# Layer two of a two-layer mixture of experts: four weight gathers issued one at a time, a later gate product, and a last strip in three slices

## The chip, the cores and the metric

One core of one Trainium2 chip runs the whole program. The metric is device time in microseconds of one execution. A core has a tensor engine (TensorE, PE in the profile), a vector engine (VectorE, DVE), a scalar engine (ScalarE, ACT), GpSimd (POOL) and a queue engine (SyncE, SP); each runs its own instructions in order, and they wait for one another by semaphores. Transfers run on the core's 16 DMA engines. In this kernel SP issues the plain and transposing transfers and POOL the indirect ones (gathers and scatters).

## The reference, cut to what matters

```python
def reference(**kwargs):
    attn_out = _attn_ref(**attn_kwargs)            # (4, 8, 576, 64), local and strided masks
    x = attn_out.transpose(0, 2, 1, 3).reshape(2304, 512)
    x = _moe_ref(x=x, **moe_kwargs)                # layer one: every token through all 8 experts
    return _moe2_ref(x=x, **moe2_kwargs)           # layer two: every token through one expert

def _moe2_ref(x, w_gate, w1, w2):                  # N = 2304, D = 512, E = 8, F = 1024
    cap = N // E                                   # 288 tokens for each expert
    logits = x @ w_gate
    order = np.argsort(-logits.flatten())
    for idx in order:                              # greedy: best free (token, expert) pair first
        tok, e = idx // E, idx % E
        if assigned[tok] >= 0 or counts[e] >= cap:
            continue
        assigned[tok] = e
        counts[e] += 1
    for e in range(E):
        h = np.maximum(x[assigned == e] @ w1[e], 0.0)
        out[assigned == e] = h @ w2[e]
    return out
```

The greedy assignment is done in rounds. A round (`route`) finds which expert fills up next, by a search over the sorted keys, and closes it. So the order of the experts is known only while the kernel runs, and each expert's weights and rows are fetched by indirect transfers whose index a round has computed.

## The kernel before, in words

Products in both layers work on pairs of two-byte values: a number is split into a high and a low part, and a product is three matmuls (high with high, low with high, high with low).

**Layer one, and the gate product.** Most of the time goes to layer one's experts. `Sides` runs side work between PE's matmuls by planned time: a generator yields (DVE time, ACT time, planned wait), and is taken up again when the planned clock has passed the wait. One of these generators is `late_tiles`, which begins with `late_w`: it multiplies the last expert's second weight with layer two's gate weight, in 8 pieces, adds the two parts (line 1265), takes the largest magnitude of each partition (line 1267) and passes it to `power_max`, whose matmul (line 1040) spreads it over the partitions. The result scales the product, and the last expert of layer one uses it. PE's order is fixed by hand there, so that matmul stands at the place where the generator's wait of 2.5 put it.

**Layer two.** `ffn` runs eight expert phases of 288 rows, in the order in which the rounds deliver the experts. A phase has two parts:
- eight strips `f` of the first product: 12 matmuls of 288 columns (line 1719), then a Relu on ScalarE out of PSUM (line 1724), a copy on ScalarE that makes the high part (line 1725), and a subtraction on VectorE that makes the low part (line 1726);
- four output strips `d` of the second product: 24 matmuls of 288 columns (line 1752) and a copy out of PSUM on ScalarE (line 1760).

In strips 1 to 3 of a phase, `ffn_y` finishes the phase before: for each of three blocks of 96 rows four transposes on PE (line 1692), a scaling copy on ScalarE (line 1694) and a scatter to the output issued by POOL (line 1695). The last phase's three blocks follow behind its last strip.

**Weights and rows of the next expert.** There are three sets of weight buffers, `w3`; phase `ph` uses set `ph % 3` and fetches for phase `ph + 1`. `load_w2` (line 1605) issues four indirect gathers, one for each weight part: high and low of w1, high and low of w2, each 128 rows of 4096 two-byte values. It is called once in a phase, after the first strip at which the next expert's index `wis[ph + 1]` is there (at the latest in strip 5). The rows come by `ffn_g` (three gathers of 96 rows, `g`), called at output strip 1, and go through transposing transfers on SP into `xg` (line 1635), which the next phase's first matmul reads. For phases 6 and 7 PE transposes them instead (line 1639, `ptg`).

**Order of the work.** PE's order in layer two is written out by hand: the program's own order, with the routing's matmuls (`pcnt`, `pany`, `pgg`, `pidx`) put between the strips' matmuls by fixed waits. The other engines' orders are chosen when the program is built, from the dependencies and modelled times. POOL's gathers of weights depend on the index and on nothing of the phase in which they are called. The matmuls' banks in PSUM (`mm`) come from four buffers, the transposes' from two.

Of the kernel before, what the change touches and what calls it, by code (L numbers as in the profile page):

```python
# [13 lines left out]
AF = mybir.ActivationFunctionType  # L14
# [4 lines left out]
N, DM, E, F = 2304, 512, 8, 1024  # L19
CAP = N // E  # L20
WIN = 32
DC = DM // 128
FC = F // 128
# [52 lines left out]
LATE_AT = 8  # L76
DIRECT = 14, 15
TURNED = range(1, 6)


class Arena:
# [14 lines left out]
    def part(self, shape, dt):  # L96
        n = math.prod(shape[1:]) * mybir.dt.size(dt)
        n = (n + 31) // 32 * 32
        r = next(x for x in self.room if x[1] + n <= x[0].shape[1] * 2)
        o, r[1] = r[1] // 2, r[1] + n  # L100
        v = r[0][:shape[0], o:o + n // 2]
        v = (v if dt == F16 else v.bitcast(dt))[:, 0:math.prod(shape[1:])]
        names = "abcd"[:len(shape) - 1]
        return v if len(shape) == 2 else v.rearrange(f"p ({' '.join(names)}) -> p {' '.join(names)}",
                                                     **dict(zip(names[1:], shape[2:])))
# [132 lines left out]
class Kernel:  # L238
# [21 lines left out]
    def bank(self, name, tag="bank"):  # L260
        tag = tag if tag in self.banks else "l1"
        return self.psum.tile([128, 512], F32, name=name, tag=tag, bufs=self.banks[tag])
# [985 lines left out]
    def late_w(self):  # L1248

        nc = self.nc  # L1250
        while ("moe", E - 1, 1) not in self.sides.done:
            yield 0, 0, 0.5
        self.lwp = self.m2.tile([128, FC, 2 * E], F32, name="lwp")
        for c in range(FC):
            t = self.m2.tile([128, 2 * DC, 128], F16, name="turned")
            for k in range(2):
                nc.sync.dma_start(out=t[:, k * DC:k * DC + DC], in_=self.w7d[k][:, c * DM:c * DM + DM], transpose=True)
            yield 0, 0, 8.0
            ps = self.bank("pl", "l1")
            self.gate_dot(ps, (t, t[:, DC:]))  # L1260
            yield 0, 0, 1.0
            nc.scalar.activation(self.lwp[:, c], ps[:, 0:2 * E], AF.Copy)
            yield 0, 0.3, 0
        v = self.lwp[:, :, 0:E]
        nc.vector.tensor_tensor(v, v, self.lwp[:, :, E:], op=OP.add)
        mx = self.sm.tile([128, 1], F32, name="gmx")
        nc.vector.tensor_reduce(mx, v, axis=AX.XY, op=OP.max, apply_absolute_value=True)
        yield 0.5, 0, 2.5
        yield from self.power_max(mx)
        s, self.lwi = self.pow2_scale(self.m2, 8.0, self.top, "lscale")  # L1270
        self.lw = self.m2.tile([128, FC, 2 * E], F16, name="lw")
        self.w_split(v, s[:, 0:1], self.lw[:, :, 0:E], self.lw[:, :, E:])
        yield 1.0, 0, 0
# [328 lines left out]
                t = next(routes, None)  # L1602
                self.wait = 1e9 if t is None else self.wait + t

    def load_w2(self, ph):
        for k in range(4):
            self.nc.gpsimd.indirect_dma_start(out=self.w3[ph % 3][k].rearrange("p a b -> p (a b)"), out_offset=None,
                                              in_=self.wd[k],
                                              in_offset=bass.IndirectOffsetOnAxis(ap=self.wis[ph][:, :1], axis=0))

    def ffn_g(self, ph):

        nc = self.nc
        idx = self.places[ph][0]
        gs = []
        for s in range(3):
            if ph:
                g = self.fp.tile([96, XR], F16, name=f"g{s}")
            else:
                g = self.r0.tile([96, XR], F16, name=f"g{s}", bufs=1)  # L1620
            nc.gpsimd.indirect_dma_start(out=g, out_offset=None, in_=self.xd,
                                         in_offset=bass.IndirectOffsetOnAxis(ap=idx[:, s:s + 1], axis=0))
            gs.append(g)
        self.gs[ph] = gs

    def ffn_x(self, ph, s):
# [6 lines left out]
        xg, osc = self.fx[ph]  # L1633
        if ph in TURNED:
            nc.sync.dma_start(out=xg[:, :, s * M:s * M + M], in_=gs[s][:, 0:2 * DM], transpose=True)
# [66 lines left out]
    def ffn(self, routes):  # L1702

        nc, fp = self.nc, self.fp
        bank = lambda: self.bank("mm", "l1")[:, :CAP]
        for ph in range(E):
            w = self.w3[ph % 3]
            if ph + 1 < E:
                loaded = False
            xg = self.fx[ph][0]  # L1710
            hh = fp.tile([128, FC, CAP], F16, name="h2h")
            hl = fp.tile([128, FC, CAP], F16, name="h2l")
            for f in range(FC):
                ps = bank()
                fs = slice(f * 128, f * 128 + 128)
                k = 0
                for d in range(DC):
                    for l, r in ((w[0], d), (w[0], DC + d), (w[1], d)):
                        nc.tensor.matmul(ps, l[:, d, fs], xg[:, r], start=k == 0, stop=k == 3 * DC - 1)  # L1719
                        k += 1  # L1720
                    if d == 1:
                        yield
                r = fp.tile([128, CAP], F32, name="h2", bufs=5)
                nc.scalar.activation(r, ps, AF.Relu)
                nc.scalar.activation(hh[:, f], r, AF.Copy)
                nc.vector.tensor_tensor(hl[:, f], r, hh[:, f], op=OP.subtract)
                yield
                if ph and 0 < f < 4:
                    self.ffn_y(ph - 1, f - 1)
                if ph + 1 < E and not loaded:  # L1730
                    if f == 5:
                        self.until_has(self.wis, ph + 1, routes)
                    if len(self.wis) > ph + 1:
                        self.load_w2(ph + 1)
                        loaded = True
            yt = self.fy[ph] = fp.tile([128, DC, CAP], F32, name="yt")
            for d in range(DC):
                if ph + 1 < E and d == 1:
                    self.until_has(self.places, ph + 1, routes)
                    if ph + 1 not in self.gs:  # L1740
                        self.ffn_g(ph + 1)
                    if ph + 1 in TURNED:
                        for n in range(3):
                            self.ffn_x(ph + 1, n)
                if ph + 1 < E and ph + 1 not in TURNED and d == 3:
                    self.ffn_x(ph + 1, 1)
                ps = bank()
                dsl = slice(d * 128, d * 128 + 128)
                k = 0
                for f in range(FC):  # L1750
                    for l, r in ((w[2], hh), (w[3], hh), (w[2], hl)):
                        nc.tensor.matmul(ps, l[:, f, dsl], r[:, f], start=k == 0, stop=k == 3 * FC - 1)  # L1752
                        k += 1
                    if f % 2 and f < FC - 1:
                        if ph + 1 < E and ph + 1 not in TURNED and (d, f) in ((2, 5), (3, 3)):
                            self.ffn_x(ph + 1, 2 * d - 4)
                        if ph + 1 == len(self.places) < min(len(self.wis), E):
                            self.spare()
                        yield
                nc.scalar.activation(yt[:, d], ps, AF.Copy)  # L1760
                yield
        for s in range(3):
            self.ffn_y(E - 1, s)

    def layers(self):
        tc, nc = self.tc, self.nc
# [236 lines left out]
```

## Time and profile before

| | |
|---|---|
| time, median of 3 runs | 1873.65 us (1871.69 to 1874.94) |
| the profiled execution | 1867.06 us |
| its span in the trace | 1864.9 us |
| TensorE busy | 1783.4 us, 96% of the span |
| VectorE, ScalarE, GpSimd busy | 60%, 49%, 30% |
| mean rate of the DMA queues | 127 GB/s |
| bytes of POOL's indirect transfers (queue 0) | 43.01 MB |

The span runs from the first to the last instruction in the trace; the device time holds the start and the end around it, 2.2 us here. Shares of busy time are means over the whole span. Layer two's expert phases lie between about 1594 and 1852 us.

### The profile page before, as it was taken

What the parts mean: (1) busy time and instruction counts of PE and PEld (TensorE: products, weight loads), DVE (VectorE), ACT (ScalarE), POOL (GpSimd) and SP (SyncE); (2) the same over time, 40 slices, a digit from 0 to 9 for tenths busy, and PEclk for the clock granted to TensorE, in tenths of its full rate; (3) what the DMA queues carried; (4) which work ended last, traced back from release to release, by engine and by line L of the source; (5) the groups of instructions that cost most, each with busy time, mean ns of one, the idle gap of its engine ahead of it and who ended that gap; (6) DMA issues with size and microseconds to landing.
All of it is one profiled execution on the core that took longest, in us unless ns stands there. A gap on an engine that the chain in (4) does not pass through costs nothing.

```text
span 1864.9 us, 32915 instructions
## 1 busy us (share of the span) xinstructions
PE 1783.4 (96%) x12741; PEld 1081.7 (58%) x12741; DVE 1125.2 (60%) x2706; ACT 907.3 (49%) x2145; POOL 550.2 (30%) x557
## 2 busy tenths in 40 slices
PE   6899999999999999999999999999999999888897
PEld 4666765555455555555554555555556764676776
DVE  6744458866766475566536664666545668766630
ACT  5655533563575456456724744376735531232243
POOL 2121202240442134232402331233356513232231
PEclk8899999999999999999999999999999999999999
DMA  8121012232474046406742542466531113465460
GB/s 265 40 70 41 26 46 80 95 125 109 160 238 155 34 158 226 136 35 204 225 125 88 185 132 99 151 205 201 161 113 35 35 46 130 136 200 169 147 232 26
DMA packets 116561, 237.16 MB, mean 127 GB/s; under 512 B 48620, under 2 KB 53300, under 8 KB 108180
## 3 DMA queue, kind: packets, MB, share of 16 engines
q1 hardware_dynamic: 108724, 192.05, 32.1%
q0 software_dynamic: 7680, 43.01, 6.4%
q8 instruction: 100, 1.64, 0.4%
q14 instruction: 57, 0.47, 0.1%
HBM read 160.75 MB, written 64.50 MB: 121 GB/s over the span
## 4 chain that ended last, share of the span: by engine, by line
PE 60%; issue 15%; DVE 12%; ACT 5%; DMA 4%; POOL 2%; another core or an unknown queue 1%; SPq 0%; POOLq 0%; ACTq 0%; DVEq 0%
PE l L1103 22%; PE l L1159 16%; PE l L679 7%; PE mm L1719 3%; PE l L661 3%; PE mm L1752 3%; DVE w1s L547 2%; POOL raw L1012 1%; ACT sm L417 1%; DVE wmx L1059 1%; DMA raw<-in_moe_w_dram 1%; PE po L458 1%; PE pcnt L1384 1%; PE ps L392 1%; DMA ws0h<-m2h 1%
## 5 line engine op out<-in xcount | busy, mean ns | idle before, releaser
L1103 PEld LDWEIGHTS <-w1s 128*128 128x128 f16 x3864 | 370.2, 98 | 210.9 <-issue 4.2
L1103 PE MATMUL l<-sx,w1s 128*128 128x384 f16 (+2 forms) x2208 | 337.3, 312 | 1.3 <-ACT vV L1118 1.1
L1159 PE MATMUL l<-w2h,hl 128*128 128x512 f16 x864 | 327.4, 379 | 0.0
L1159 PE MATMUL l<-w2l,hh 128*128 128x512 f16 x864 | 327.4, 379 | 0.0
L1159 PE MATMUL l<-w2h,hh 128*128 128x512 f16 x864 | 327.4, 379 | 0.0
L551 POOL TENSOR_TENSOR m2l<-raw,m2h 128x512 f16<-128x512 f32 x176 | 206.3, 1173 | 398.6 <-ACT raw L550 348.5
L1159 PEld LDWEIGHTS <-hh 128*128 128x128 f16 x1728 | 167.7, 98 | 197.4
L1103 PE MATMUL l<-xh,w1s 128*128 128x384 f16 (+2 forms) x1104 | 258.7, 312 | 3.5 <-DVE hl L951 2.0
L711 DVE SCALAR_TENSOR_TENSOR acc<-l,pe,acc 128x512 f32<-128x512 f32 x126 | 94.1, 748 | 180.1 <-PE l L1159 154.1
L1012 POOL TENSOR_TENSOR raw<-raw 128x256 f32<-128x256 f32 x112 | 100.0, 896 | 323.1 <-DVE w1s L547 243.6
L1059 DVE TENSOR_REDUCE wmx<-raw 128x1 f32<-128x512 f32 x240 | 152.0, 677 | 45.4 <-DMA raw<-in_moe_w_dram 44.9
L1103 PE MATMUL l<-xl,w1s 128*128 128x384 f16 (+2 forms) x552 | 171.3, 312 | 0.0
L549 ACT ACTIVATE m2h<-raw,wscale 128x512 f16<-128x512 f32 x176 | 125.3, 712 | 91.1 <-DVE wscale L287 36.6
L1159 PEld LDWEIGHTS <-hl 128*128 128x128 f16 x864 | 84.5, 98 | 102.0
L1118 ACT ACTIVATE vV<-l 128x384 f32<-128x384 f32 x144 | 68.4, 488 | 132.3 <-PE l L1103 131.5
L550 ACT ACTIVATE raw<-raw,wscale 128x512 f32<-128x512 f32 x176 | 127.0, 722 | 5.7
L679 PE MATMUL l<-w2h,hl 128*128 128x512 f16 x288 | 110.6, 384 | 0.0
L679 PE MATMUL l<-w2h,hh 128*128 128x512 f16 x288 | 110.5, 384 | 0.0
L679 PE MATMUL l<-w2l,hh 128*128 128x512 f16 x288 | 110.4, 383 | 0.0
L428 POOL TENSOR_TENSOR sm<-sm,den 96x768 f32<-96x768 f32 (+1 forms) x32 | 42.7, 1335 | 186.5 <-DVE den L427 115.9
L547 DVE SCALAR_TENSOR_TENSOR w1s<-raw,wscale,w1s 128x512 f16<-128x512 f32 x96 | 81.7, 895 | 16.3 <-ACT w1s L546 16.2
L546 ACT ACTIVATE w1s<-raw,wscale 128x512 f16<-128x512 f32 x96 | 57.6, 658 | 66.4 <-POOL raw L1012 48.5
(395 smaller groups left out, 2995.1 us busy)
## 6 DMA issues: line engine op xcount, KB each, us to landing
raw<-in_moe_w_dram SPq DMA_DIRECT2D x120, 512.0 KB, 5.6
sx<-sd SPq DMA_DIRECT2D x15, 1536.0 KB, 7.5
wd<-m2h SPq DMA_DIRECT2D x64, 256.0 KB, 3.5
wd<-m2l SPq DMA_DIRECT2D x64, 256.0 KB, 3.4
kq<-in_qk_dram SPq DMA_DIRECT2D x16, 592.0 KB, 3.8
sd<-sx SPq DMA_DIRECT2D x3, 1536.0 KB, 5.6
acc<-in_moe_w_dram SPq DMA_DIRECT2D x2, 2048.0 KB, 10.5
w1s<-wl SPq DMA_DIRECT2D x4, 896.0 KB, 5.8
```

What stands on the lines that cost most here:

```text
L546: nc.scalar.activation(hi, raw, AF.Copy, scale=s)
L547: nc.vector.scalar_tensor_tensor(lo, raw, s, hi, op0=OP.mult, op1=OP.subtract)
L549: nc.scalar.activation(hi, raw, AF.Copy, scale=s)
L550: nc.scalar.activation(raw, raw, AF.Copy, scale=s)
L551: nc.gpsimd.tensor_tensor(lo, raw, hi, op=OP.subtract)
L679: nc.tensor.matmul(ps, l[:, f, js], r[:, f], start=k == 0, stop=k == 3 * FC - 1)
L711: self.last = [nc.vector.scalar_tensor_tensor(a, ps, pe[:, c:c + 1], a, op0=OP.mult, op1=OP.add).ins]
L1012: nc.gpsimd.tensor_tensor(o, x, y, op=OP.subtract)
L1059: nc.vector.tensor_reduce(mx[:, 2 * q + k:2 * q + k + 1], part(q)[:, k * 512:k * 512 + 512], axis=AX.X, op=OP.max, apply_absolute_value=True)
L1103: self.nc.tensor.matmul(ps, self.w1s[:, fs, x, k, d], a[y][:, d], start=first and m == 0, stop=m == 5, skip_group_check=not first)
L1118: copy = lambda o, i: nc.scalar.activation(o, i, AF.Copy)
L1159: nc.tensor.matmul(ps, l[:, f, js], r[:, f], start=k == 0, stop=k == 3 * FC - 1)
```

## The change

Three edits:

1. **The gathers.** Where `load_w2` was called, the four parts are now only put on a list. A counter `since` grows by 1 after each strip of the first product and by 2 ahead of each output strip; whenever it has reached `GAP` = 3 and the list isn't empty, one gather is issued and the counter goes back to 0. The first goes at once. What is left at the end of the phase is issued there. Each gather is given a dependency on the last ScalarE copy (`copied`: of a strip's high part, or of an output strip), so that POOL waits for it.
2. **The gate product.** In `late_w` the planned wait between the maximum and `power_max` is 8.0 in place of 2.5.
3. **The end.** The last output strip of the last phase is done in three slices of 96 columns: 24 matmuls each, then a copy of the slice. The block of the slice before is finished (`ffn_y`) behind the second and the third slice's matmuls, the last block behind that.

```diff
+GAP = 3
 ...
-        yield 0.5, 0, 2.5
+        yield 0.5, 0, 8.0
         yield from self.power_max(mx)
 ...
-    def load_w2(self, ph):
-        for k in range(4):
-            self.nc.gpsimd.indirect_dma_start(out=self.w3[ph % 3][k].rearrange("p a b -> p (a b)"), out_offset=None,
+    def load_w2(self, ph, parts=range(4), after=None):
+        for k in parts:
+            st = self.nc.gpsimd.indirect_dma_start(out=self.w3[ph % 3][k].rearrange("p a b -> p (a b)"), out_offset=None,
                                               in_=self.wd[k],
                                               in_offset=bass.IndirectOffsetOnAxis(ap=self.wis[ph][:, :1], axis=0))
+            if after is not None:
+                self.tc.add_manual_dep(st.ins, after.name, mybir.DependencyInfo(
+                    mybir.DependencyClass.Sync, mybir.DependencyReason.DATA), reason="spread")
 ...
+        parts, since = [], 0
+
+        def part(n):
+            nonlocal since
+            since += n
+            if parts and since >= GAP:
+                self.load_w2(ph + 1, (parts.pop(0),), self.copied)
+                since = 0
 ...
-                nc.scalar.activation(hh[:, f], r, AF.Copy)
+                self.copied = nc.scalar.activation(hh[:, f], r, AF.Copy).ins
 ...
-                        self.load_w2(ph + 1)
+                        parts, since = list(range(4)), GAP
                         loaded = True
+                part(1)
             yt = self.fy[ph] = fp.tile([128, DC, CAP], F32, name="yt")
             for d in range(DC):
+                part(2)
 ...
+                if ph == E - 1 and d == DC - 1:
+                    for s in range(3):
+                        m = slice(s * 96, s * 96 + 96)
+                        for f in range(FC):
+                            for l, r in ((w[2], hh), (w[3], hh), (w[2], hl)):
+                                nc.tensor.matmul(ps[:, m], l[:, f, dsl], r[:, f, m], start=k == 0, stop=k == 3 * FC - 1)
+                                k += 1
+                        k = 0
+                        nc.scalar.activation(yt[:, d, m], ps[:, m], AF.Copy)
+                        if s:
+                            self.ffn_y(ph, s - 1)
+                    self.ffn_y(ph, 2)
+                    return
 ...
-                nc.scalar.activation(yt[:, d], ps, AF.Copy)
+                self.copied = nc.scalar.activation(yt[:, d], ps, AF.Copy).ins
                 yield
-        for s in range(3):
-            self.ffn_y(E - 1, s)
+            while parts:
+                part(GAP)
```

## Rows read from the trace of the kernel before

**Rows 1.** Windows: start:end, length, busy us of each engine, PE clock, DMA share, GB/s.
```profile
800.00:1200.00 400.00, 396.70 (x2183) 208.03 (x2181) 233.81 (x433) 205.93 (x391) 107.57 (x105) 1.00 0.44 143
...
1600.00:1800.00 200.00, 178.22 (x1911) 141.85 (x1910) 125.26 (x586) 58.05 (x132) 61.74 (x63) 0.96 0.60 197
```

**Rows 2.** Windows: six stretches of layer two, then the sum of those between.
```profile
1611.00:1620.00 9.00, 7.21 (x74) 5.24 (x71) 4.97 (x19) 0.41 (x1) 2.79 (x3) 0.81 0.80 304
1641.00:1648.00 7.00, 3.33 (x41) 2.25 (x40) 3.46 (x13) 2.34 (x6) 0.94 (x1) 1.00 0.96 375
1675.00:1680.00 5.00, 2.59 (x33) 1.46 (x32) 3.61 (x12) 2.63 (x7) 0.93 (x1) 1.00 1.02 378
1707.00:1720.00 13.00, 9.65 (x92) 6.38 (x91) 4.64 (x14) 3.16 (x8) 1.88 (x2) 0.74 0.66 253
1743.00:1750.00 7.00, 3.82 (x42) 2.39 (x40) 2.86 (x10) 2.79 (x7) 2.31 (x3) 1.00 0.97 363
1777.00:1788.00 11.00, 7.99 (x54) 5.40 (x53) 2.72 (x9) 4.26 (x11) 5.63 (x6) 0.69 0.90 340
...
sum 155.00, PE 150.44 PEld 124.23 DVE 106.72 ACT 44.96 POOL 47.27; mean PE 18.81 PEld 15.53 DVE 13.34 ACT 5.62 POOL 5.91
```

**Rows 3.** Timeline of POOL, expert phase 3: start, us, line, operation, [idle before <-releaser].
```profile
1700.74 0.97 POOL L1607 DMA_INDIRECT acc<-wd,raw  x1 [13.40 <-issue]
...
1704.52 1.05 POOL L1607 DMA_INDIRECT acc<-wd,raw  x1 [0.31 <-issue]
1705.87 1.02 POOL L1607 DMA_INDIRECT acc<-wd,raw  x1 [0.30 <-issue]
...
1708.45 0.94 POOL L1695 DMA_INDIRECT out_dram<-y,raw  x1 [0.30 <-issue]
```

**Rows 4.** Timeline of PE and ACT in the same stretch.
```profile
1703.02 4.33 PE L1719 MATMUL mm<-xg,xh 128*128 128x288 f16 x34
...
1709.96 0.28 PE L1719 MATMUL mm<-xg,xh 128*128 128x288 f16 x1 [0.42 <-issue]
...
1710.73 0.41 ACT L1724 ACTIVATE h<-mm 128x288 f32<-128x288 f32 x1 [5.06 <-remote]
...
1714.37 0.19 PE L1390 MATMUL pany<-w1s,first 128*128 128x40 bf16 x1 [1.27 <-DVE w1s L1386]
```

**Rows 5.** Windows: two stretches with the DMA engines full.
```profile
1022.00:1026.00 4.00, 4.00 (x20) 1.84 (x19) 2.16 (x4) 0.00 (x0) 0.00 (x0) 1.00 0.99 368
...
1788.00:1801.00 13.00, 12.85 (x132) 10.65 (x130) 3.61 (x19) 3.79 (x7) 4.72 (x5) 1.00 0.92 350
```

**Rows 6.** Windows and PE's timeline: the end of expert phase 1.
```profile
1654.00:1660.00 6.00, 5.02 (x61) 4.11 (x60) 3.81 (x15) 0.82 (x2) 0.81 (x1) 1.00 0.95 156
1660.00:1666.00 6.00, 6.00 (x83) 5.06 (x82) 3.84 (x17) 1.75 (x5) 0.00 (x0) 1.00 0.05 10
...
1661.86 0.90 PE L1719 MATMUL mm<-xg,w1s 128*128 128x288 f16 x6
```

**Rows 7.** Timeline at the gate product's maximum.
```profile
1009.77 0.22 DVE L1267 TENSOR_REDUCE gmx<-lwp 128x1 f32<-128x64 f32 x1
...
1010.04 0.23 PE L1040 MATMUL amx<-identb,gmx 128*128 128x128 bf16 x1 [2.49 <-DVE gmx L1267]
```

**Rows 8.** Timeline of the end.
```profile
1852.37 0.41 ACT L1760 ACTIVATE yt<-mm 128x288 f32<-128x288 f32 x1 [2.53 <-PE mm L1752]
...
1853.19 1.26 ACT L1694 ACTIVATE y<-pty,osc 96x512 f32<-96x512 f32 x2 [0.41 <-PE pty L1692]
...
1854.14 0.92 POOL L1695 DMA_INDIRECT out_dram<-y,raw  x1 [17.20 <-ACT y L1694]
...
1856.60 0.92 POOL L1695 DMA_INDIRECT out_dram<-y,raw  x1 [0.30 <-issue]
```

**Rows 9.** Timeline of PE: transposes of 96 columns, and what follows.
```profile
1825.53 0.51 PE L1639 MATMUL ptg<-identh,g 96*128 96x96 f16 x8
...
1825.87 0.41 PE L1752 MATMUL mm<-h2h,xl 128*128 128x288 f16 x2
```

## The prediction

> **What bounds the kernel now.** I read the windows by stage first. In the middle of the first layer TensorE (PE) is busy 396.70 of 400 us at full clock; in the 200 us in which layer two runs its experts 0 to 5 it is busy 178.22, at a mean clock of 0.96 [rows 1]. So there is little to win outside this stage and some 30 us of room in it. Next I cut that stage where the DMA share stands near 1. In six stretches, 52 us in all, PE is busy 34.59 and idle 17.4 us (by row 1.8, 3.7, 2.4, 3.4, 3.2, 3.0). [...] Lost in the six: 3.5 + 3.7 + 2.4 + 6.7 + 3.2 + 6.4 = 25.9 us. The 155 us between them lose 4.6 us of PE time, 3% [rows 2].
>
> What is in those stretches: GpSimd (POOL) issues the four weight gathers of the next expert in a line, 1.3 us apart, with the scatters of y around them [rows 3]. Each carries 128 rows of 4096 two-byte values, 1.05 MB, at the 363 to 378 GB/s of the full stretches [rows 2] some 2.8 us, so four keep the DMA engines full for about 11 us. The timeline of that stretch shows what it does. PE starts 34 matmuls at a pitch of (4.33-0.29)/33 = 0.122 us, then goes on one by one, 0.42 us idle ahead of 0.28 each, with nothing that it waits for by the profile. ScalarE's next Relu comes after an idle time of 5.06 us, at 1710.73, and then the routing's matmul waits 1.27 us for VectorE, which had stood behind the same copies [rows 4]. All three engines stop together and start again about 1.3 us after POOL's last issue (1708.45 + 0.94) [rows 3, 4]. Which resource they lack the trace doesn't say. A full DMA alone doesn't do it: at 1022 to 1026 the share is 0.99 with PE busy all 4 us, and at 1788 to 1801, when expert 7's gathers land in a run without routing, PE is busy 12.85 of 13 [rows 5].
>
> **The gathers, spread.** The same gathers are issued by the same engine; what moves is when. Each now waits for a ScalarE copy, and the counter gives the distance: a strip of the first product counts 1, one of the second 2, at 3 the next gather goes. With the strip at which the routing delivers the index, as its matmuls stand between the strips in PE's timeline, they go out behind strips 3, 6, 7 and output strip d1 in expert phase 0; 2, 5, 7 and d1 in phase 1; 1, 4, 7 and d0 in phases 2 and 3; 0, 3, 6 and 7 in phases 4 to 6. Three strips are 36 matmuls or 4.4 us at 0.122, longer than the 2.8 us of one gather; strips 6 and 7 are 1.5 us apart, so two gathers still overlap there. Terms:
> - Phases 1, 2, 3 hold no such pair: their whole loss comes back, 3.7 + 2.4 + 6.7 = 12.8 us.
> - Phases 0, 4, 5 keep a pair, half the bunch; I take half their loss back: (3.5 + 3.2 + 6.4)/2 = 6.5. Bounds: nothing, and all of the 13.1.
> - The stretches then lose what the rest of the stage does, 3% of some 26 us of work: 0.8 us.
> - In phases 0 and 1 the fourth gather now flies beside the row gathers g and the transposes that make xg for the next expert. In phase 1 those keep the DMA busy until about 1660 (share 0.95, then 0.05), and the next expert's first matmul is at 1661.86 [rows 6]: 1.9 us of slack against 2.8 us more traffic, so about 1 us late, twice: 2 us. Bounds: none, and 2.8 us in each of six phases, 17 us.
> Sum: 12.8 + 6.5 - 0.8 - 2 = 16.5 us returned; bounds 0 and 25.9 - 0.8 = 25.1.
>
> The new wait sits on POOL's queue, in order. Behind a waiting gather stand y's scatters, which nothing on PE needs soon, and the g gathers, which xg needs; that is the 2 us above. The last two weights of a set are used only in the second product, eight strips or 11.8 us into the next phase, so a fourth gather that ends late in a phase has that cover. Issue costs on POOL stay (32 x about 1 us, off the path). The extra semaphore on ScalarE's copy I cost at nothing.
>
> [...]
>
> **The gate product.** The chain's matmul L1040 waited 2.49 us for VectorE's maximum, which ended at 1009.99; 5.5 planned microseconds later it finds it done [rows 7]. Nothing else moves but the scale behind it, which only the last expert of layer one uses. PE is busy 99% around it [rows 1], so the time is passed on: 2.4 us. Bounds 0 (a later wait swallows it) and 2.5.
>
> **The end.** Before, the last strip's matmuls end at about 1852.34, its copy of 0.41 us starts at 1852.37, then y is scaled from 1853.19 and the three scatters go out 1.23 us apart, issue bound, the last at 1856.60 [rows 8]. After, the last strip is done in three column slices of 24 matmuls of 96 columns. The nearest row is eight 96-column transposes in 0.34 us (1825.53 to 1825.87), 0.0425 us each [rows 9]: 72 take 3.06 instead of 2.93 us. The first slice's four transposes (0.44 us, by the pitch of 0.12) stand before the third slice, which so ends at 1852.3 + 0.1 + 0.4 = 1852.8. The first y is then scaled at about 1852.1, and its scatter follows 0.95 us later as before, 1853.05; the second slice's y starts at 1853.35, its scatter at 1854.3, the third at 1855.5: 1.1 us earlier. Bounds: 0, if copies and matmuls of one PSUM bank hold each other up (two copies of up to 0.41 us), and 1.3.
>
> **Sum.** 16.5 + 2.4 + 1.1 = 20 us. The profiled execution took 1867.06 (span 1864.9); less 20 it is 1847. The median of the runs shown is 1873.65, 0.35% above it; I put the same 20 us on the median: **1853.7 us**.
>
> **Rivals.**
> - *The bytes do it, not the bunch.* Each gather keeps its share of the stop and only the gate and the end gain: 3.5 us, with 0 to 3 from the spread: 1867 to 1870. For it: the stops fall where the DMA is full. Against: the two full stretches without loss [rows 5], and the stops begin only some microseconds into a line of issues. [...]
> - *Slower: every lone gather brings a stop of its own.* 24 gathers in phases 0 to 5 instead of six bunches. If one costs more than (25.9 + 3.5)/24 = 1.2 us the change loses; at 1.6 us it is 38.4 - 29.4 = 9 us slower, 1883. For it: after an idle stretch the clock stays low for a while (0.74 over 13 us), which small stops could bring on again. Against: ScalarE and PE go on normally for 3 us and more after the first gather of a line.
> - *xg late in every phase.* A weight gather on POOL's queue ahead of g costs 2.8 + 1 us; less 1.9 of slack, 1.9 us in each of six phases, 11 us instead of 2: 1863. For it: in phases 2 and 3 the fourth gather is in the program just before g. Against: it waits for a copy that comes when g's index does.
>
> **How the numbers follow.** As forecast (8 to 25 us back from the spread): 0.70, its own range 1845 to 1862. Bytes: 0.15. Slower: 0.07. xg late: 0.08. The 8-in-10 range reaches from the full return (25.1 + 2.5 + 1.3 = 29, 1845) to the upper part of the first rival: 1845 to 1867. What a measurement here can tell from no change is 0.2%, 3.7 us: faster 0.70 + 0.08 + 0.09 of the first rival = 0.87; same 0.07; slower 0.06.
>
> **What would show it.** Right: in the after profile POOL's weight gathers stand apart with ScalarE's copy as their releaser; no matmuls one by one on PE and no 5 us idle before a Relu; phases 0 to 5 shorter by 2 to 6 us each, at full clock; no 2.49 us at L1040; a last scatter 1.1 us nearer to the last matmul. Wrong: PE waits on a DMA at a phase's first matmul (xg late), pany waits for VectorE as long as before though the gathers are apart (the routing chain bounds the stage), or a stop of a microsecond after every gather.

## The result, and the profile after

| | before | after |
|---|---|---|
| median of the comparison, us | 1873.55 (6 runs) | 1854.95 (6 runs) |
| ratio, 95% interval | | 0.9905 [0.989, 0.992] |
| the profiled execution, its span | 1867.06, 1864.9 | 1852.00, 1850.2 |

The time is 1.2 us from the forecast and within its range. How it comes about is another matter, and the experiments below put a condition on it: on another Trainium2 chip the same change made the kernel slower.

The profiled execution of before is 6.5 us below its median and that of after 3.0 below its own, so the traces show 14.7 us of the medians' 18.6. Against the traces the forecast of 20 us is 5 too high; that the median came out 1.2 us from it is in part luck. I cut the spans at two steps of ScalarE that both kernels have: the first Relu of expert phase 0 (1597.11 before, 1595.02 after) and the copy of phase 5's last output strip (1801.67, 1787.42). Up to the first, 2.1 us are won; behind the second, 37.4 us to the end of the span became 36.9 (1850.2 - 1787.42 less phase 6's 25.86, and so before); between them, in phases 0 to 5, 12.2. Windows of that stretch, before:

```profile
1597.11:1801.67 204.56, 182.60 (x1960) 145.39 (x1959) 127.64 (x592) 60.56 (x137) 61.74 (x63) 0.96 0.59 193
```

After, with two of its phases (0 and 2, cut at their first matmul):

```profile
1595.02:1787.42 192.40, 178.18 (x1960) 144.74 (x1959) 127.48 (x592) 60.75 (x138) 58.64 (x60) 0.98 0.62 185
...
1592.15:1627.71 35.56, 31.37 (x349) 24.65 (x349) 23.05 (x108) 8.05 (x19) 6.65 (x7) 0.93 0.54 153
...
1660.61:1696.95 36.34, 31.90 (x358) 25.59 (x359) 21.99 (x100) 9.93 (x23) 9.65 (x10) 0.95 0.61 166
```

TensorE's idle time fell from 22.0 to 14.2 us, and its busy time by 4.4, at a mean clock of 0.98 in place of 0.96. But 14.2 us idle is far from none, and phases 0 and 2 are longer than in the kernel before (33.04 and 33.77, from first matmul to first matmul). The stops themselves are gone. TensorE's timeline at phase 3's gathers, which answers to [rows 4]:

```profile
1704.33 5.31 PE L1731 MATMUL mm<-xg,xh 128*128 128x288 f16 x42
```

42 matmuls run on without a gap where before 34 ran and the rest came one by one. What took the place of the stops is on GpSimd. Its timeline in phase 2 after, answering to [rows 3] (L1608 weights, L1625 g):

```profile
1672.50 0.97 POOL L1608 DMA_INDIRECT xh<-wd,raw  x1 [0.30 <-issue]
1675.67 0.96 POOL L1608 DMA_INDIRECT xl<-wd,raw  x1 [2.19 <-ACT h2h L1737]
1679.75 0.92 POOL L1625 DMA_INDIRECT g<-xd,raw  x1 [3.12 <-DVE raw L1568]
1680.98 1.14 POOL L1608 DMA_INDIRECT xl<-wd,raw  x1 [0.30 <-issue]
1682.42 0.92 POOL L1625 DMA_INDIRECT g<-xd,raw  x1 [0.30 <-issue]
1683.65 0.92 POOL L1625 DMA_INDIRECT g<-xd,raw  x1 [0.30 <-DVE w1s L1387]
```

The weights stand apart, but the fourth one went out between the first and the second row gather. TensorE's waits in layer two, after (engine, line, what it waited for; us in total, times, longest):

```profile
PE pcnt L1385 <- DVE w1s L1379: 5.2, 8, 2.1
PE pany L1391 <- DVE w1s L1387: 4.7, 7, 2.6
PE pany L1391 <- DVE osc L1645: 2.3, 2, 1.2
PE mm L1731 <- DMA xg<-g: 1.7, 1, 1.7
PE mm L1769 <- ACT yt L1772: 0.3, 1, 0.3
```

12.2 us for the routing's steps on VectorE, 1.7 for xg. The same steps of the kernel before:

```profile
PE pany L1390 <- DVE w1s L1386: 10.7, 10, 2.5
...
PE pcnt L1384 <- DVE w1s L1378: 1.5, 3, 0.8
```

That is 12.2 us too, so these waits are no shorter though the gathers stand apart.

The gate product shows at line 1041 (1040 before). The rows give the first and the last start of that line's matmuls between 905 and 1205 us. Before:

```profile
L1040 PE MATMUL amx<-identb,wmx x7: 219/219/231, 913.9 to 1192.5; 128*128 128x128 bf16 x7
```

After:

```profile
L1041 PE MATMUL amx<-identb,wmx x7: 219/219/230, 915.5 to 1192.2; 128*128 128x128 bf16 x7
```

TensorE's timeline has the gate's own matmul after, with no wait ahead of it:

```profile
1015.53 0.22 PE L1041 MATMUL amx<-identb,gmx 128*128 128x128 bf16 x1
```

The 2.49 us of [rows 7] are gone, and 278.6 us became 276.7 over the same work. The end, after, by the timelines of TensorE and GpSimd, answering to [rows 8]:

```profile
1836.49 0.24 PE L1769 MATMUL mm<-h2h,acc 128*128 128x96 f16 x2 [0.34 <-ACT yt L1772]
...
1839.11 0.91 POOL L1699 DMA_INDIRECT out_dram<-y,raw  x1 [16.43 <-ACT y L1698]
...
1841.84 0.91 POOL L1699 DMA_INDIRECT out_dram<-y,raw  x1 [0.31 <-issue]
```

From the last copy of phase 6 (1827.54 before, 1813.28 after) to the last scatter it is 29.06 us before, 28.56 after.

### The profile page after: what moved, and what is told of

Same layout as the page of the kernel before. It is cut to its first block, busy times and chain, and to the rows that moved or that the text cites. A ratio compares the mean times of both kernels' runs of the same rounds, so it can differ in the third digit from the quotient of the medians.

```text
span 1850.2 us, 33028 instructions
## 1 busy us (share of the span) xinstructions
PE 1781.5 (96%) x12789; PEld 1084.2 (59%) x12789; DVE 1125.6 (61%) x2706; ACT 906.7 (49%) x2147; POOL 550.2 (30%) x557
## 4 chain that ended last, share of the span: by engine, by line
PE 58%; issue 15%; DVE 14%; ACT 5%; DMA 5%; POOL 3%; SPq 0%; POOLq 0%; ACTq 0%; DVEq 0%
PE l L1104 22%; PE l L1160 15%; PE l L680 7%; PE l L662 3%; PE mm L1731 3%; PE mm L1779 2%; DVE w1s L548 2%; POOL raw L1013 2%; ACT sm L418 1%; DMA g<-xd,raw 1%; DMA raw<-in_moe_w_dram 1%; DVE w1s L1379 1%; DVE wmx L1060 1%; PE po L459 1%; PE ps L393 1%
```

## The experiments

They ran on four chips, and the same kernel differed more between them (26 us) than by any edit on one of them. The chip of the first comparison has no number on record, so it may be one of the four; and each chip was used once, so what belongs to the chip and what to that one occasion (how the program and its data were placed, for instance) isn't told apart. Below, a chip with stops is one on which the line of gathers stopped the engines on that occasion. "Phases" is the stretch from the first Relu to phase 5's last copy in each profiled execution.

| chip | kernel | median us | ratio to before there | phases us |
|---|---|---|---|---|
| first | before | 1873.55 | | 204.6 |
| first | after | 1854.95 | 0.9905 [0.989, 0.992] | 192.4 |
| 14 | before | 1847.58 | | |
| 14 | spreading alone | 1865.45 | 1.0081 [1.0057, 1.0106] | 198.4 |
| 14 | gate and end alone | 1842.34 | 0.9966 [0.9954, 0.9978] | 180.7 |
| 14 | rest of the weights last | 1848.14 | 1.001 [0.9995, 1.0025] | 192.3 |
| 14 | GAP = 1 | 1846.34 | 0.9999 [0.9981, 1.0017] | 185.7 |
| 9 | before, once more | 1843.92 | 0.9982 [0.9969, 0.9995] | 183.1 |
| 9 | after, again | 1855.52 | 1.0049 [1.0033, 1.0066] | 194.9 |
| 9 | gate and end alone, again | 1843.28 | 0.9981 [0.9968, 0.9994] | 181.5 |
| 9 | line of loads on SyncE | 1849.80 | 1.0009 [0.9992, 1.0027] | 192.7 |
| 5 | after, osc written later | 1859.84 | 0.9936 [0.9919, 0.9953] | 197.5 |
| 5 | gate and end, osc written later | 1870.38 | 0.9986 [0.9972, 1.0001] | 207.5 |
| 6 | line, y stored by SyncE | 1841.65 | 0.9972 [0.996, 0.9985] | 183.6 |
| 6 | line of loads on SyncE, again | 1846.16 | 1.0004 [0.9988, 1.002] | 188.9 |

On chip 9 the unchanged kernel came out at 0.9982 of itself, with an interval that leaves out 1. So a difference of 0.2% or 0.3% between two rows of this table says nothing, whatever its interval.

**The parts apart.** Spreading alone (the other two edits undone):

```diff
-        yield 0.5, 0, 8.0
+        yield 0.5, 0, 2.5
 ...
-                if ph == E - 1 and d == DC - 1:
 ...
+        for s in range(3):
+            self.ffn_y(E - 1, s)
```

> The spread gathers alone, with the old wait at the gate product and the old end. My theory (the three edits add up, and nearly all of the 18.6 us comes from the gathers): 14 to 16 us less than before, 1858 to 1860, and phases 0 to 5 as in the profile of the changed kernel. Rival (the bytes do it, and the gain came from elsewhere): at most 3 us less.

Gate and end alone (the gathers in one line again):

```diff
-                        parts, since = list(range(4)), GAP
+                        self.load_w2(ph + 1)
```

> The gate product's wait and the sliced end alone, the four gathers in a line as before. My theory: 3.5 us less than before (2.4 at the gate, 1.1 at the end), about 1870, with the stops in phases 0 to 5 unchanged. Rival (a start of layer two that is earlier by 2.4 us shifts the gathers against the matmuls and takes stops away by chance): 8 us less or more.

The first cost 17.9 us where 14 to 16 were to come back (six runs, 1856.14 to 1867.66); the second gained 5.2. On this chip the kernel before itself took 1847.58, and there was nothing to give back: in the trace of gate and end alone the line of four gathers brings no matmuls one by one. Two more runs there asked where the spreading's price is paid. After, but with what is left of the weights behind output strip 0 held to the phase's end:

```diff
             for d in range(DC):
-                part(2)
+                if d == 0:
+                    part(2)
```

> The changed kernel, but in the output strips only the one ahead of strip 0 may issue a weight gather; what is left goes at the end of the phase, behind the row gathers g and their transposes. My theory (the fourth gather among the g gathers makes VectorE wait for g and the routing behind it, in phases 0 and 2 above all, which are 2.5 us longer than before): those two phases get 3 to 5 us shorter each and the wait of VectorE for g falls from 13.8 us to below 5; 4 to 9 us less than the changed kernel. Rival (phases 0 and 2 are long for another reason): within 2 us of the changed kernel, or slower, if the late gather stops the next phase's first strips instead.

After, with the gathers behind successive strips:

```diff
-GAP = 3
+GAP = 1
```

> The changed kernel with a distance of one strip in place of three: four gathers 1.5 to 2 us apart instead of 4.4, each still behind a ScalarE copy. My theory (what counts is that one gather's 2.8 us of transfers end before the next begin): about half of the stops come back, 5 to 12 us more than the changed kernel. Rival (it is POOL's issuing back to back that stops the engines, so any pause between the issues will do): within 3 us of the changed kernel, or faster, since no gather is left among the g gathers.

After itself did not run on this chip; beside its 1855.52 on chip 9 the first is 7.4 us less, as expected, but its phases (192.3) are no shorter than after's on the first chip (192.4), and what it was to show did not come. VectorE's wait for g, which was to fall below 5 us, is

```profile
DVE osc L1645 <- DMA g<-xd,raw: 23.7, 13, 6.4
```

though no weight gather stands among the g of phases 0 to 4. Phase 0 is as long as in after on the first chip, phase 2 3.0 us shorter, phase 4 5.0 longer. So a weight gather among the row gathers isn't the whole price.

The second expectation has the wrong sign: the phases are 6.6 us shorter with GAP = 1 than with the rest held to the end, and the nearer the gathers are to a line, the shorter (185.7, against 180.7 for the line). All weights are then out well ahead of g, as the expectation's rival said; its theory, on stops, can't be tested on a chip without them.

**The same kernels on another chip.** Before, after, and gate and end alone, unchanged:

> The kernel before, unchanged, for its trace on this run's chip. Theory A (the stops of a line of four gathers come on some chips and not on others): its time and its stops go together: at 1870 us or more the trace shows ScalarE idle 4 to 5 us ahead of a Relu and matmuls one by one in phases 1 to 5, some 25 us lost by TensorE in the six stretches; at 1850 or less none of that, under 10 us lost. Theory B (the stops come and go from run to run on any chip): the time is between, 1855 to 1868, or time and stops don't go together.

> The kernel after, unchanged. Theory A: on a chip where before takes 1870 or more it is 16 to 20 us faster; where before takes about 1848 the spreading's own cost of some 15 us (the run with the spreading alone) stands against some 5 us of gate and end, 1853 to 1859, 0.3% to 0.6% slower than before. Theory B: 0.9905 again, whatever before takes.

> Gate product and end alone, four gathers in a line. Both theories: 3.5 to 5.5 us less than before on this chip, whatever before takes. If before takes 1870 or more here, this is slower than after by 13 to 16 us; if before takes about 1848, faster than after by 10 or more.

Theory A holds in all three. After takes what it took on the first chip (1855.52 and 1854.95); it is the kernel before that takes 26 us less. Its windows rows here, of the phases and of a stretch with phase 3's gathers in flight:

```profile
1595.20:1778.33 183.13, 176.19 (x1960) 144.49 (x1959) 127.71 (x592) 61.27 (x137) 64.06 (x63) 0.98 0.64 209
...
1697.00:1706.00 9.00, 8.82 (x110) 7.34 (x108) 7.04 (x27) 3.41 (x8) 5.90 (x5) 1.00 1.01 407
```

Its timeline of TensorE and GpSimd at phase 3's gathers:

```profile
1695.81 5.31 PE L1719 MATMUL mm<-xg,xh 128*128 128x288 f16 x42
...
1696.05 0.96 POOL L1607 DMA_INDIRECT acc<-wd,raw  x1 [0.30 <-PE pty L1692]
1697.32 1.05 POOL L1607 DMA_INDIRECT acc<-wd,raw  x1 [0.30 <-issue]
1698.67 1.02 POOL L1607 DMA_INDIRECT acc<-wd,raw  x1 [0.30 <-issue]
```

The same instructions at the same distances as in [rows 3], and 42 matmuls in one run where [rows 4] show 34 and then single ones; the DMA engines are as full as in [rows 2], with TensorE busy 8.82 of 9 us.

**A chip with the stops again.** The next two kernels were meant to move osc, three VectorE products that read g, from line 1645 to the next phase's first strip:

```diff
-        nc.vector.tensor_tensor(osc[:, s:s + 1], gs[s][:, 2 * DM:].bitcast(F32), self.places[ph][1][:M], op=OP.mult)
 ...
                 nc.vector.tensor_tensor(hl[:, f], r, hh[:, f], op=OP.subtract)
+                if ph and f == 0:
+                    for s in range(3):
+                        nc.vector.tensor_tensor(self.fx[ph][1][:, s:s + 1], self.gs[ph][s][:, 2 * DM:].bitcast(F32),
+                                                self.places[ph][1][:96], op=OP.mult)
```

> After, with the three small VectorE products that make osc (line 1645), which read g and so stand in VectorE's order behind a transfer, done a phase later, behind the next phase's first strip, when g has long landed. In after's two traces TensorE waits 12.2 and 10.5 us for the routing's VectorE steps, against 6.0 in the trace of gate product and end alone, and 1.7 and 3.4 us for xg. Theory A (the late g costs through VectorE's order: osc waits for g, and the routing's compares stand behind osc): 4 to 6 us less than after (1855 here and there), 1849 to 1851, the waits of pcnt and pany back to some 6 us; the wait for xg stays. Theory B (the late g costs through xg and through GpSimd's order alone): the same as after, within 2 us.

> Gate product and end alone, four gathers in a line, with osc late as well. Theory A: in this kernel g is not late, so osc holds little up: 0 to 2 us less than gate product and end alone (1842.3 and 1843.3 on two chips). Theory B: no difference. On a chip where before takes 1870 or more: some 1869, with the stops in its trace; there the run with the spreading is 13 to 18 us faster than this one.

The edit did nothing. VectorE's order is chosen when the program is built, and osc came back to where it stood, as VectorE's timeline of the first of them shows in phase 2. That phase's last copy starts at 1693.43, and osc should have come behind it:

```profile
1685.41 0.15 DVE L1740 TENSOR_TENSOR osc<-g,raw 96x1 f32<-96x1 f32 x1 [0.47 <-DMA g<-xd,raw]
1689.30 0.16 DVE L1740 TENSOR_TENSOR osc<-g,raw 96x1 f32<-96x1 f32 x1 [1.16 <-DMA g<-xd,raw]
1690.66 0.15 DVE L1740 TENSOR_TENSOR osc<-g,raw 96x1 f32<-96x1 f32 x1
```

So whether osc alone carries the price was not tested. The two runs serve as after, and as gate and end alone, on a chip where before takes 1872.09: there the spreading is worth 10.5 us (1870.38 against 1859.84; 13 to 18 were expected), and on chip 9 it costs 12.2 (1843.28 against 1855.52). With the line of gathers the stops are back, in TensorE's timeline on this chip:

```profile
1704.72 4.49 PE L1718 MATMUL mm<-xg,xh 128*128 128x288 f16 x33
1709.67 0.28 PE L1718 MATMUL mm<-xg,xh 128*128 128x288 f16 x1 [0.46 <-issue]
1710.39 0.28 PE L1718 MATMUL mm<-xg,xh 128*128 128x288 f16 x1 [0.44 <-issue]
```

**Which transfers bring the stops.** All four loads at once on SyncE, as direct transfers of expert 0's weights, and later once more; then the line on GpSimd, with y's stores on SyncE, to fixed rows:

```diff
-            st = self.nc.gpsimd.indirect_dma_start(out=self.w3[ph % 3][k].rearrange("p a b -> p (a b)"), out_offset=None,
-                                              in_=self.wd[k],
-                                              in_offset=bass.IndirectOffsetOnAxis(ap=self.wis[ph][:, :1], axis=0))
+            st = self.nc.sync.dma_start(out=self.w3[ph % 3][k].rearrange("p a b -> p (a b)"), in_=self.wd[k][0:128])
 ...
-                self.load_w2(ph + 1, (parts.pop(0),), self.copied)
+                self.load_w2(ph + 1, parts, self.copied)
+                parts.clear()
```

> After, but the four weight loads of an expert go out together behind one ScalarE copy and as direct transfers of SyncE with the rows of expert 0 (the weights are the wrong ones, the bytes are the same); GpSimd no longer issues them. If the bytes alone make the stops, it loses the same 16 to 20 us against after on a chip with stops. If GpSimd's own line of indirect transfers makes them, no stops: 1840 to 1850 on any chip, as GpSimd's queue then never holds a g gather or scatter behind a weight gather.

> The line of four weight loads as direct transfers of SyncE once more (expert 0's weights, so the output is not the reference's); it was 1849.8 on a chip where before took 1847.6. On a chip where before takes some 1872: Theory A (it is GpSimd's indirect transfers that bring the stops): 1848 to 1854, some 20 us less than before, and no matmuls one by one. Theory B (the bytes bring them, whoever issues): 1865 to 1872. On a chip where before takes some 1847: 1849 to 1851 again.

```diff
-        st = nc.gpsimd.indirect_dma_start(out=self.a["out"],
-                                          out_offset=bass.IndirectOffsetOnAxis(ap=idx[:, s:s + 1], axis=0),
-                                          in_=y, in_offset=None)
+        row = ph * CAP + s * M
+        st = nc.sync.dma_start(out=self.a["out"][row:row + M], in_=y)
 ...
-                self.load_w2(ph + 1, (parts.pop(0),), self.copied)
+                self.load_w2(ph + 1, parts, self.copied)
+                parts.clear()
```

> After, but the four gathers of an expert go out together behind one ScalarE copy, and y's blocks are stored by SyncE with direct transfers to fixed rows (the output's rows are permuted), so that no scatter of GpSimd stands among the gathers. In the trace of before the stops are in phases 1 to 5, in which scatters stand among the gathers, and not in phase 0 and at expert 7's gathers, where none do. On a chip where before takes some 1872: Theory A (a stop needs gathers and scatters of GpSimd together): no stops, 1845 to 1855. Theory B (the line of gathers is enough): stops as in before, 1864 to 1870. On a chip where before takes some 1847 both expect 1840 to 1848, and nothing is told apart.

All three ran on chips where before takes 1846 to 1848. There are no stops there to take away, so they leave the question open; their times are within 3 us of what was expected there. What they do show is that without stops a line of direct loads on SyncE is no better than the line on GpSimd (1849.80 against 1843.28 on chip 9).

## Why the prediction was right, and where it was not

**The stops: right in mechanism, for some chips.** On the first chip and on chip 5 the line of four gathers stops the engines, and spreading removes the stops. I take their price as the difference between the same phases with and without: 204.6 - 183.1 = 21.4 us for the kernel before, first chip against chip 9; the prediction read 25.9 - 0.8 = 25.1 from [rows 2]. Most of the difference is phase 0: the prediction read 3.5 us there, but the trace of before has no matmuls one by one in it, and without stops it is only 1.0 us shorter. Of the prediction's 25.9, 17.4 is idle time; the other 8.5 (1.7, 3.4 and 3.4 in the first, fourth and sixth stretch) was the author's estimate of what the lowered clock cost, from its means there (0.81, 0.74 and 0.69), and no run shows that term. What the runs showed in its place: in the trace of before the granted clock is 0.50 from 1616 to 1619, from 1712 to 1718 and from 1780 to 1786, and TensorE's busy time in the phases is 6.4 us above that on chip 9 (182.60 against 176.19). Each phase from its first matmul to the next one's, in us:

| kernel, chip | 0 | 1 | 2 | 3 | 4 | 5 |
|---|---|---|---|---|---|---|
| before, first | 33.04 | 34.28 | 33.77 | 36.99 | 34.63 | 34.22 |
| after, first | 35.56 | 32.90 | 36.34 | 31.25 | 30.80 | 28.22 |
| before, 9 | 32.06 | 29.90 | 33.40 | 30.46 | 31.02 | 28.22 |
| gate and end, 9 | 32.22 | 30.45 | 30.57 | 30.90 | 31.08 | 28.23 |
| after, 9 | 34.16 | 34.57 | 34.80 | 34.16 | 31.28 | 28.25 |
| rest of the weights last, 14 | 35.53 | 30.92 | 33.30 | 31.16 | 35.84 | 28.23 |

That a chip could be without the stops was in no rival.

**Its signs.** Of those that were to show it right, the stops and the 2.49 us are gone; but the phases were to be 2 to 6 us shorter each, and on the first chip only 3, 4 and 5 are (5.7, 3.8 and 6.0), phase 1 by 1.4, and 0 and 2 are 2.5 and 2.6 us longer, at a mean clock of 0.93 and 0.95. Of those that were to show it wrong, two came beside the gain: TensorE waits for xg once (1.7 us), and the routing's waits are as long as before (12.2 us).

**The fraction returned.** The prediction took back 19.3 of the 25.9, because the pair of gathers behind strips 6 and 7 was to keep half a bunch. After's trace has no matmuls one by one anywhere in layer two, so I take all of the 21.4 to have come back, not three quarters; a comparison across chips, not a measurement.

**The failed step: "2 us" for the gather that flies beside g.** This term was mis-sized, and by more than the point above. On a chip without stops the spreading has nothing to give back, and it lengthens the phases from 181.5 to 194.9 us (chip 9, gate and end alone against after). On the first chip after's 192.4 is 9.3 above the 183.1 that the kernel before takes where it doesn't stop. So 9 to 13 us, not 2: 21.4 - 9.3 = 12.2 is what the first chip gave. The two errors stood against each other, and the 16.5 of the prediction is only 4 us above that; that is luck. The prediction counted phases 0 and 1. On chip 9 phases 0 to 3, in which the fourth gather goes out beside or behind the g, are 1.9, 4.1, 4.2 and 3.3 us longer than in gate and end alone; 4 and 5 are within 0.2, though in 5 two gathers stand among the g. The split isn't sharp: on chip 14 spreading alone is 3.0, 4.4, 7.0, 0.9, 2.6 and 0.3 us longer, phase by phase, than gate and end alone.

Part of what the step had overlooked can be read in the trace of after on chip 9. GpSimd's timeline puts the fourth weight gather of phase 2 at 1684.20, right behind the first g (1682.97), and the other two g at 1685.64 and 1686.88. The timeline of TensorE and VectorE, from the start of that phase:

```profile
1662.69 1.31 PE L1731 MATMUL mm<-xg,w1s 128*128 128x288 f16 x6 [3.37 <-DMA xg<-g]
...
1687.99 0.15 DVE L1645 TENSOR_TENSOR osc<-g,raw 96x1 f32<-96x1 f32 x1 [2.68 <-DMA g<-xd,raw]
1688.07 0.25 DVE L1394 TENSOR_SCALAR_CACHE_REDUCE w1s<-pany,w1s 128x39 f32<-128x39 f32 x1
...
1688.85 1.10 DVE L1379 SCALAR_TENSOR_TENSOR w1s<-w1s,zero,jt 128x400 bf16<-128x400 f32 x2
...
1689.54 0.82 PE L1385 MATMUL pcnt<-w1s,sx 128*128 128x40 bf16 x18 [1.55 <-DVE w1s L1379]
```

osc waits 2.68 us for g, the routing's search stands behind osc in VectorE's order, and TensorE waits for the search. The prediction followed g to xg alone (the first row, 3.37 us at the start of phase 2; 1.7 on the first chip, near the 2 that it said). It didn't ask who else reads g. TensorE's waits of the two kernels on chip 9 sum it up, after:

```profile
PE pcnt L1385 <- DVE w1s L1379: 6.3, 9, 1.6
PE pany L1391 <- DVE w1s L1387: 4.2, 4, 2.1
PE mm L1731 <- DMA xg<-g: 3.4, 1, 3.4
PE mm L1731 <- ACT yt L1787: 1.4, 2, 0.9
```

and gate and end alone:

```profile
PE pcnt L1384 <- DVE w1s L1378: 4.0, 6, 1.4
PE pany L1390 <- DVE w1s L1386: 2.0, 3, 1.1
```

15.3 against 6.0 us. The windows rows of the two, after first, add the clock (0.97 against 0.99): 179.25 us busy in place of 175.01.

```profile
1596.46:1791.38 194.92, 179.25 (x1960) 145.60 (x1959) 127.17 (x592) 61.34 (x137) 59.40 (x60) 0.97 0.64 182
```

```profile
1597.65:1779.17 181.52, 175.01 (x1960) 143.88 (x1959) 127.59 (x592) 61.35 (x138) 64.44 (x63) 0.99 0.65 211
```

9.2 us more idle and 4.2 us more busy are the 13.4 of difference.

The lateness of g isn't all of it either. VectorE's order differs between the two kernels as they are built, and in the spread one osc stands further ahead. Phase 0 of after on the first chip, VectorE and TensorE:

```profile
1619.67 0.15 DVE L1645 TENSOR_TENSOR osc<-g,raw 96x1 f32<-96x1 f32 x1 [2.59 <-DMA g<-xd,raw]
1619.75 0.25 DVE L1387 TENSOR_SCALAR w1s<-pcnt,sx 128x39 bf16<-128x39 f32 x1
...
1620.05 0.18 PE L1391 MATMUL pany<-w1s,first 128*128 128x39 bf16 x1 [2.60 <-DVE w1s L1387]
```

and VectorE in phase 0 of before, on the same chip:

```profile
1620.91 0.26 DVE L1386 TENSOR_SCALAR w1s<-pcnt,sx 128x39 bf16<-128x39 f32 x1 [1.07 <-PE pcnt L1384]
1621.08 0.15 DVE L1641 TENSOR_TENSOR osc<-g,raw 96x1 f32<-96x1 f32 x1
```

In after two osc stand ahead of the search's step of line 1387, which waits with them; in before the step goes first and the first osc behind it finds g there. The fourth gather of this phase went out only behind all three g (1617.47), so it is not what they waited behind. How much of the price each carries, osc's place in the built order, the later g, and the transfers of xg, stays open, as the run that should have told them apart changed nothing.

Whether a small g issued behind a weight gather lands later for it the traces show only in part. On chip 9 the row gathers of phase 2 and the transposing transfers that read them (one view holds both) landed 4.2 to 5.6 us after their issue with the weight gather among them, and 2.9 to 3.5 in gate and end alone; but in the kernel before, with the same line, the same phase has 2.9 to 6.3. On the same chip phase 1's transposing transfers landed after at most 9.3 us with the spreading and after at most 4.6 in gate and end alone.

**The gate product.** Forecast 2.4; 1.9 measured between the matmuls of line 1041. Right.

**The end.** Forecast 1.1; 0.5 measured. What the prediction named for its bound happened once: the second slice's matmuls waited for the first slice's copy out of the same PSUM bank (0.34 us idle, and the start at 1836.49 is 0.54 behind the last matmul of the first slice at 1835.95).

**Gate and end in the medians.** 5.2, 4.3 and 1.7 us on three chips, where the traces give 2.4. With an unchanged kernel coming out 3.6 us below itself, the medians can't say more than that the sum is small and not a loss.

**The rivals.** "Slower: every lone gather brings a stop" is false: no stops in any trace of a spread kernel. The low clock behind an idle stretch, which spoke for it, shows in three of the six stretches of [rows 2] (0.81, 0.74 and 0.69); the other three, with 2.4 to 3.7 us idle, are at 1.00. "xg late in every phase", at 11 us in all, was near the price, and began at the right place, a g behind a weight gather; but the wait for xg that it named came once in each of after's traces (1.7 and 3.4 us). "The bytes, not the bunch" is false on the chips with stops, since the same bytes spread give no stops. On the chips without, there is nothing to give back, so they say nothing on it.

**What stays open.** Which resource stops all engines at once, and why on some chips (or on some occasions) alone. The profile shows one more difference between the two kinds of chip. DMA issues on chip 9, kernel before (operation, times, median us from issue to landing):

```profile
g<-xd,raw POOLq DMA_INDIRECT x21, 3.8
...
acc<-wd,raw POOLq DMA_INDIRECT x12, 9.5
```

and on chip 5, gate and end with osc written later:

```profile
g<-xd,raw POOLq DMA_INDIRECT x21
acc<-wd,raw POOLq DMA_INDIRECT x12
```

On the first chip and on chip 5, in all four traces, no landing of g or of acc is recorded in layer two; on chips 14, 9 and 6 they are, in each of the eight traces of kernels in which GpSimd fetches the weights. The records of these transfers' ends are missing on the chips where the line stops the engines, also in after's trace, which has no stops. The trace can't say whether both have one cause.

## What to carry to other kernels

Before a large transfer is put among small ones on a queue, list every instruction that reads the small ones: here one reader was a product of 0.15 us on VectorE, and the routing's search stood behind it in order. Then compare that order in the two kernels as built, since an edit of one engine's waits can move it. A gain read from one trace is a gain on that chip: after is 18.6 us faster than before on the first chip, 12.2 on chip 5 (the kernel in which osc was to move) and 8.0 slower on chip 9, so the unchanged kernel belongs among the kernels measured, on several chips. GAP = 1 has phases between those of the two versions on chip 14 (1846.34 us in all), and did not run on a chip with stops.

## What the runs showed of the hardware that was not expected

- The same program took 1873.55 and 1872.09 us on the first chip and chip 5, and 1847.58, 1847.55 and 1845.86 on chips 14, 9 and 6, at mean clocks of 0.985 and 0.988 in the two profiled executions of it. Most of the difference is in TensorE's idle time in phases 0 to 5, 22.0 against 6.9 us, and in its busy time, 182.60 against 176.19.
- The kernel with the spread gathers took 1854.95 and 1855.52 us on one chip of either kind, and 1859.84 on chip 5 with the edit that moved nothing.
- The line of gathers is the same on both kinds: four issues 1.3 us apart, and DMA engines that are full behind them (a share of 1.01 at 407 GB/s in the stretch above, on a chip without stops; 0.96 to 1.02 at 363 to 378 GB/s in three of the stretches of [rows 2]).
